# Linear attention and a gated MLP on one core: next chunk's x fetched as soon as it is written, first batch in the steady order, its last normalizers inverted on VectorE

## The chip, the cores and the metric

The kernel runs on one core of a Trainium2 chip. The metric is device time in microseconds (us), as the median of several runs; lower is better. A core has a matrix engine (TensorE, PE in the profile; its weight loads are PEld), VectorE (DVE), ScalarE (ACT), GpSimd (POOL) and SyncE (SP), each with an instruction queue of its own that is executed in order. In this kernel SP issues every DMA; a transfer that has to wait for something holds up SP's queue behind it.

## The reference

Attention with a feature map and without a softmax over the sequence, followed by a gated MLP over all tokens. There are 8 batches, 8 heads, 576 positions, head size 64, 128 features; the MLP has 4608 tokens, width 512 and hidden width 1536.

```python
def phi(x):
    proj = np.einsum('bhsd,df->bhsf', x, w_phi)
    proj = proj - np.max(np.abs(proj), axis=-1, keepdims=True)
    return np.concatenate([np.exp(proj), np.exp(-proj)], axis=-1)
q_p, k_p = (phi(q), phi(k))
kv = np.einsum('bhsf,bhsd->bhfd', k_p, v)
z = np.sum(k_p, axis=2)
num = np.einsum('bhsf,bhfd->bhsd', q_p, kv)
den = np.einsum('bhsf,bhf->bhs', q_p, z)[..., None] + 1e-06
attn = num / den
...
gate = 1.0 / (1.0 + np.exp(-(x @ w_gate)))
val = x @ w_val
out = gate * val @ w_out
```

Here x is attn with the heads of a token side by side (4608 x 512).

## The kernel before

The first part of the program does the attention and a third of the MLP side by side; the second part does the other two thirds of the MLP and is not touched by the change.

**Attention.** Two heads make a pair, so there are 32 pairs, four to a batch. For each pair, `keys` and `rest` project k on PE, `k_exp` takes the maxima and differences on DVE and the exponentials on ACT; `q_half` projects q in two halves, `q_max` finds each position's maximum on DVE (a reduction with a transpose, some small copies and a transpose back) and subtracts it, `q_exp` exponentiates on ACT; `kv` multiplies the keys' features by v and sums them, `turn` transposes the result, and `num` (L569 to L596) computes numerators (`nm`) and denominators (`dp`). `norm` (L598 to L634) then inverts the denominators: a DMA gathers them into a tile of 128 x 9 (`dn`), DVE adds 1e-6 and inverts, a DMA writes them to DRAM (`den`), two DMAs read them back spread over all partitions (`rb`), DVE multiplies (`xp`), and the product goes to DRAM in the layout of x (`xscr`, shown as `xs`). For the first batch `norm` also splits the product into a high and a low part, straight into the x tiles of chunks 0 and 1 in SBUF.

**The MLP's first third.** The tokens are cut into 18 chunks of 256, and the hidden width into 12 blocks, of which this part does four. For each chunk c and block i, `half(c, i, m)` does the 12 matmuls of the gate (m = 0) or of the value (m = 1) into a `gv` bank; each product of two f32 values is made of three matmuls of high and low parts. `gate` makes the hidden tile, and `half_out` multiplies it by the output weights. From chunk 2 on, `load_x` (L202 to L211) reads the chunk's x from `xscr` by one DMA into the low tile, waits three ticks, casts the high part on ACT (L208), waits one, and subtracts on DVE (L210). There are two sets of x tiles.

**Order.** In this part the order of the instructions on every engine is that of the program. Work that needs several steps is a generator in a list, `tasks`; `start` runs its first step and each `tick` runs one more step of every task in the list, so a `yield` puts later steps behind what other tasks issue. `fill` (L664) is called four times a pair. It makes three ticks, and between them runs as many items of MLP work as its budget allows: what is ready, spread over the calls that are left until more is due, at most `RATE` a call. `queue(b)` enters the chunks that batch b completes, right after the numerators of the batch's last pair, and sets their due call: two calls on for the first batch, eight for the others (`LAG`). At that call the chunks' items join the list of ready work; `chunk(c)` and `first` also enter the chunk in the set `cs`. `begin(c)` (L213) starts `load_x(c)` if c is in `cs` and hasn't been started; it is called at the start of `half`, which then ticks until the x tile is complete, and after the second half of every block but the first, for chunk c+1.

**The first batch** has a loop of its own (L709 to L740): for pair i it projects keys and queries of pair i+1, then does `q_exp`, `kv`, `turn` and `num` of pair i one after another. The later pairs run in the loop at L742, where `num(i-1)` stands between `kv(i)` and `turn(i)`.

**Weights** come as 64-bit floats and are taken apart on DVE and ACT, twelve tiles in this part; `grant(n)` lets the task `weigh` go on up to tile n, and `need` makes `half` wait for the tile it reads.

Of the kernel before, what the change touches and what calls it, by code (L numbers as in the profile page):

```python
# [36 lines left out]
EARLY = NP  # L37
RATE = 2.8
LAG = (2, 8)
TICKS = 3  # L40


@with_exitstack
def attention_moe(
# [144 lines left out]
    def start(g):  # L189

        if next(g, tasks) is not tasks:
            tasks.append(g)

    def tick():
        for g in list(tasks):
            if next(g, tasks) is tasks:
                tasks.remove(g)

    def half_units(js, mp, ps_gv, ps_acc, need):
        xs, hs, gvs, cs, parts = {}, {}, {}, set(), collections.Counter()  # L200

        def load_x(c):  # L202
            xh, xl, raw = x_tiles(mp, CH, f"1_{c}")
            xs[c] = xh, xl
            nc.sync.dma_start(raw, xscr[c])
            for _ in range(3):
                yield
            act.copy(xh, raw)  # L208
            yield
            vec.tensor_tensor(xl, raw, xh.bitcast(F32), op=ALU.subtract)  # L210
            parts[c] = NP  # L211

        def begin(c):  # L213
            if c in cs and c not in xs:
                start(load_x(c))

        def gate(c, i, n):
            gv = gvs.pop((c, i))
            u = mp.tile([P, CH], F32, tag="u", name="u" + n)
            t = mp.tile([P, CH], F32, tag="t", name="t" + n)  # L220
            hh = mp.tile([P, CH], F32R, tag="hh", name="hh" + n, bufs=10)
            hl = mp.tile([P, CH], F32R, tag="hl", name="hl" + n, bufs=10)
            hs[c, i] = hh, hl, None
            act.activation(t, gv[:, 0, :], AF.Tanh, scale=0.5)
            act.activation(u, gv[:, 0, :], AF.Exp)
            yield
            tu = t.bitcast(U32)
            vec.tensor_scalar(tu, tu, 0x7FFFFFFF, None, op0=ALU.bitwise_and)
            vec.scalar_tensor_tensor(t, t, 1.0, gv[:, 1, :], op0=ALU.add, op1=ALU.mult)
            vec.scalar_tensor_tensor(u, u, 1.0, t, op0=ALU.min, op1=ALU.mult)  # L230
            yield
            act.copy(hh, u)  # L232
            yield
            vec.tensor_tensor(hl, u, hh.bitcast(F32), op=ALU.subtract)  # L234
            parts["h", c] += 1

        def half(c, i, m):
            begin(c)
            while parts[c] < NP:
                tick()  # L240
            need(js[i], m)
            n = f"1_{c}_{js[i]}"
            if m == 0:
                gvs[c, i] = ps_gv.tile([P, 2, CH], F32, tag="gv", name="gv" + n)
            mm_in(gvs[c, i][:, m, :], xs[c], js[i], m, CH)
            if m == 1:
                start(gate(c, i, n))
                if i >= 1:
                    begin(c + 1)

        def half_out(c, t):
            need(js[-1], 2)
            while parts["h", c] < len(js):
                tick()
            acc = ps_acc.tile([P, DM], F32, tag="acc", name=f"acc1_{c}_{t}")
            for i, j in enumerate(js):
                mm_out(acc, t, hs[c, i], j, i == 0, i == len(js) - 1)
            y = mp.tile([P, DM], F32, tag="y", name=f"y1_{c}_{t}")
            act.activation(y, acc, AF.Copy, scale=0.5)

            def store():
                yield
                nc.sync.dma_start(yscr[c][t], y)

            start(store())

        def unit(c, i):
            return [(1.45, lambda m=m: half(c, i, m)) for m in range(2)]

        def chunk(c):  # L270

            cs.add(c)
            items = []
            for i in range(len(js)):
                items += unit(c, i)
                if i < 2:
                    items += outs(c - 1)[i : i + 1]
            return items

        def first():  # L280

            cs.update((0, 1))
            items = []
            for i in range(len(js)):
                items += unit(0, i) + unit(1, i)
            return items + outs(0)

        def outs(c):
            return [(0.69 * len(js), lambda t=t: half_out(c, t)) for t in range(2)]

        return chunk, first, outs, xs, parts

    def rest_chunks(js, xp, mp, ps_gv, ps_acc, load):
        def load_x(C):
# [57 lines left out]
    with ExitStack() as actx:  # L352
# [9 lines left out]
        def bank(shape, name):  # L362
            return ps_a.tile(shape, F32, tag="a", name=name)
# [202 lines left out]
                yield  # L566
            exps[i] = es

        def num(i):  # L569
            es, w = exps.pop(i), kvs.pop(i)  # L570
            ex = at.tile([P, S], F32, tag="ex", name=f"ex{i}")
            nms = [bank([P, HS], f"nm{i}_{hf}") for hf in range(2)]
            dp = bank([P, HS], f"dp{i}")
            for hf in range(2):
                cs = slice(hf * HS, hf * HS + HS)
                for sg in range(2):
                    for o in range(0, P, Q):
                        nc.tensor.matmul(  # L578
                            nms[hf][o : o + Q, :], w[:, sg, o : o + Q],
                            es[sg][:, o // D, cs],  # L580
                            start=sg == 0, stop=sg == 1, tile_position=(0, o),
                        )
            for sg in range(2):
                for o in range(0, P, Q):
                    hd, hf = divmod(o // Q, 2)
                    z = (2 * hd + sg) * Q
                    nc.tensor.matmul(  # L587
                        dp[o : o + Q, :], w[:, 2, z : z + Q],
                        es[sg][:, hd, hf * HS : hf * HS + HS],
                        start=sg == 0, stop=sg == 1, tile_position=(0, o),  # L590
                    )
            dr = at.tile([P, HS], F32, tag="dr", name=f"dr{i}", bufs=1)
            for hf in range(2):
                act.copy(ex[:, hf * HS : hf * HS + HS], nms[hf])
            act.copy(dr, dp)
            start(norm(i, ex, dr))  # L596

        def norm(i, ex, dr):  # L598
            b, p = steps[i]
            dn = at.tile([P, 9], F32, tag="dn", name=f"dn{i}")  # L600
            rb = at.tile([P, S], F32, tag="rb", name=f"rb{i}", bufs=1)
            yield
# [5 lines left out]
            yield  # L608
            nc.sync.dma_start(dens[i].rearrange("h (r c) -> (h r) c", c=9), dn)
            yield  # L610
            for hd in range(2):
                nc.sync.dma_start(
                    rb[head(hd), :], dens[i][hd].unsqueeze(0).broadcast_to([D, S])
                )
            for _ in range(3):
                yield
            xp = at.tile([P, S], F32, tag="xp", name=f"xp{i}")
            vec.tensor_tensor(xp, ex, rb, op=ALU.mult)
            for c in range(S // CH if b == 0 else 0):
# [8 lines left out]
            while t < S:  # L628
                c, o = divmod(b * S + t, CH)
                w = min(CH - o, S - t)  # L630
                nc.sync.dma_start(
                    xscr[c][:, p * CH + o : p * CH + o + w], xp[:, t : t + w]
                )
                t += w  # L634

        weighed = []
# [4 lines left out]
                grant(3 * j + m + 1)  # L641
                tick()

        chunk, first, outs, xs, parts = half_units(list(range(JA)), moe, ps_gv, ps_acc, need)
        ready, coming = [], []
        cdone = wdone = spot = after = 0
        wq = []
# [16 lines left out]
        def fill(n=TICKS):  # L664
            nonlocal due, spot, after
            spot += 1
            while coming and coming[0][0] <= spot:
                b, cs = coming.pop(0)[1:]
                after = spot + 4 * NP + (0 if b else 6 + LAG[1] - LAG[0])
                if b == 0:  # L670
                    ready.extend(first())
                else:
                    for c in cs:
                        ready.extend(chunk(c))
# [31 lines left out]
            load_v(i)  # L706
        start(weigh())

        keys(0)  # L709
        copies(q_half(0, 0))  # L710
        tick()
        copies(q_half(0, 1))
        rest(0)
        start(q_max(0))
        for _ in range(4):
            tick()
        for i in range(EARLY):
            more = i + 1 < EARLY
            if more:
                keys(i + 1)  # L720
                copies(q_half(i + 1, 0))
            start(q_exp(i))
            tick()
            tick()
            kv(i)
            tick()
            if more:
                copies(q_half(i + 1, 1))
                rest(i + 1)
                start(q_max(i + 1))  # L730
            tick()
            turn(i)
            load(i + 2)
            load_v(i + 2)
            tick()
            tick()
            num(i)
            tick()
            tick()
            grant((0, 1, 2, 6)[i])  # L740
        queue(0)
        for i in range(EARLY - 1, N + 1):  # L742
            if EARLY <= i:
# [108 lines left out]
```

## Time and profile before

| What | us |
|---|---|
| median of 3 runs (1372.89 to 1375.34) | 1373.25 |
| the profiled execution, whole | 1375.71 |
| its span in the profile | 1373.9 |
| TensorE busy | 1240.4 |
| VectorE busy | 793.9 |
| ScalarE busy | 528.5 |

The profile is that of one execution, and its times of instructions belong to that one. A busy line gives an engine's time and its share of the span. Lines of a timeline give the start, the time, the engine, the line of the program, the operation and the tiles written and read, with the number of instructions merged; in square brackets stands how long the engine had been idle before, and what ended that idle time. A line of waits gives an engine and line, the engine and line it waited for, the total, the number of waits and the longest. The granted clock is the share of full speed at which TensorE was let run; 1.00 is full.

### The profile page before, as it was taken

What the parts mean: (1) busy time and instruction counts of PE and PEld (TensorE: products, weight loads), DVE (VectorE), ACT (ScalarE), POOL (GpSimd) and SP (SyncE); (2) the same over time, 40 slices, a digit from 0 to 9 for tenths busy, and PEclk for the clock granted to TensorE, in tenths of its full rate; (3) what the DMA queues carried; (4) which work ended last, traced back from release to release, by engine and by line L of the source; (5) the groups of instructions that cost most, each with busy time, mean ns of one, the idle gap of its engine ahead of it and who ended that gap; (6) DMA issues with size and microseconds to landing.
All of it is one profiled execution on the core that took longest, in us unless ns stands there. A gap on an engine that the chain in (4) does not pass through costs nothing.

```text
span 1373.9 us, 22434 instructions
## 1 busy us (share of the span) xinstructions
PE 1240.4 (90%) x9104; PEld 975.0 (71%) x9104; DVE 793.9 (58%) x1606; ACT 528.5 (38%) x1082; POOL 0.7 (0%) x6
## 2 busy tenths in 40 slices
PE   6656986979979999797987999999999999999998
PEld 4334654757757777575687888888888888888887
DVE  6689774875858777587279495243434343424333
ACT  5435554645535565463444342221212221212211
POOL 0000000000000000000000000000000000000000
PEclk9968898989989999898999999999999999999999
DMA  4566232323323333232276362020202020201010
GB/s 152 170 227 206 93 107 92 116 88 100 117 79 112 113 117 100 76 112 66 67 240 209 129 207 92 0 93 1 92 0 92 0 93 1 92 26 67 1 62 31
DMA packets 81303, 131.84 MB, mean 96 GB/s; under 512 B 18608, under 2 KB 38192, under 8 KB 81200
## 3 DMA queue, kind: packets, MB, share of 16 engines
q1 hardware_dynamic: 81200, 130.41, 29.0%
q8 instruction: 72, 1.18, 0.4%
q14 instruction: 31, 0.25, 0.1%
HBM read 92.33 MB, written 28.46 MB: 88 GB/s over the span
## 4 chain that ended last, share of the span: by engine, by line
PE 70%; DVE 17%; DMA 7%; ACT 3%; issue 2%; SPq 1%; DVEq 0%
PE acc L170 19%; PE g L163 14%; PE v L163 14%; PE gv L163 10%; PE kvz L528 3%; PE nm L578 3%; DMA den<-dn 2%; DMA rb<-den 2%; PE dp L587 2%; DMA wraw<-w_moe 2%; DVE d L518 2%; PE pq L411 1%; DVE pm L500 1%; DVE mb L513 1%; PE pk L421 1%
## 5 line engine op out<-in xcount | busy, mean ns | idle before, releaser
L163 PE MATMUL gv<-xh,wh 128*128 128x256 f32 x576 | 178.3, 310 | 47.0 <-ACT xh L208 24.8
L163 PE MATMUL gv<-xl,wh 128*128 128x256 f32 x576 | 171.7, 298 | 28.1 <-DVE xl L210 28.1
L170 PE MATMUL acc<-wh,hh 128*128 128x512 f32 x432 | 172.8, 400 | 1.7 <-ACT hh L232 1.0
L163 PE MATMUL gv<-xh,wl 128*128 128x256 f32 x576 | 170.9, 297 | 0.0
L170 PE MATMUL acc<-wh,hl 128*128 128x512 f32 x432 | 169.1, 391 | 1.1 <-DVE hl L234 0.9
L170 PE MATMUL acc<-wl,hh 128*128 128x512 f32 x432 | 169.3, 392 | 0.0
L163 PEld LDWEIGHTS gv<-xh,wh 128*128 128x128 f32 x576 | 117.8, 205 | 65.5 <-ACT xh L208 25.8
L163 PEld LDWEIGHTS gv<-xl,wh 128*128 128x128 f32 x576 | 118.0, 205 | 30.3 <-DVE xl L210 29.7
L61 ACT CAST hh<-u 128x512 fp32r<-128x512 f32 x72 | 44.7, 621 | 228.4 <-DVE u L184 228.4
L182 DVE TENSOR_SCALAR t<-t 128x512 uint32<-128x512 uint32 x72 | 30.6, 426 | 166.9 <-ACT t L179 166.9
L163 PEld LDWEIGHTS gv<-xh,wl 128*128 128x128 f32 x576 | 118.2, 205 | 0.0
L163 PE MATMUL g<-xh,wh 128*128 128x512 f32 x288 | 113.0, 392 | 0.0
L163 PE MATMUL v<-xh,wh 128*128 128x512 f32 x288 | 112.6, 391 | 0.0
L163 PE MATMUL g<-xh,wl 128*128 128x512 f32 x288 | 112.5, 391 | 0.0
L163 PE MATMUL g<-xl,wh 128*128 128x512 f32 x288 | 112.5, 391 | 0.0
L163 PE MATMUL v<-xl,wh 128*128 128x512 f32 x288 | 112.3, 390 | 0.0
L163 PE MATMUL v<-xh,wl 128*128 128x512 f32 x288 | 112.1, 389 | 0.0
L179 ACT ACTIVATE t<-g 128x512 f32<-128x512 f32 x72 | 43.0, 597 | 175.5 <-PE g L163 175.2
L183 DVE SCALAR_TENSOR_TENSOR t<-t,v 128x512 f32<-128x512 f32 x72 | 49.4, 686 | 96.5 <-PE v L163 96.5
L170 PEld LDWEIGHTS acc<-wh,hh 128*128 128x128 f32 x432 | 81.4, 188 | 24.3 <-issue 4.8
L170 PEld LDWEIGHTS acc<-wh,hl 128*128 128x128 f32 x432 | 81.3, 188 | 21.0 <-DVE hl L234 2.5
L454 ACT ACTIVATE ek<-dk 128x512 f32<-128x512 f32 (+1 forms) x192 | 87.6, 519 | 19.6 <-DVE dk L445 18.8
(90 smaller groups left out, 2106.0 us busy)
## 6 DMA issues: line engine op xcount, KB each, us to landing
wraw<-w_moe SPq DMA_DIRECT2D x36, 512.0 KB
xl<-xs SPq DMA_DIRECT2D x34, 512.0 KB
k<-k SPq DMA_DIRECT2D x32, 320.0 KB
v<-v SPq DMA_DIRECT2D x32, 320.0 KB
q<-q SPq DMA_DIRECT2D x32, 288.0 KB
rb<-den SPq DMA_DIRECT2D x64, 144.0 KB
wh<-wtop SPq DMA_DIRECT2D x36, 256.0 KB
ys<-y SPq DMA_DIRECT2D x36, 256.0 KB
```

What stands on the lines that cost most here:

```text
L61: a = act.copy(h, x)
L163: nc.tensor.matmul(o, a[:, ws], x[:, cs], start=i == 0, stop=i == 11)
L170: nc.tensor.matmul(acc, a[:, ts], w[:, ws], start=first and i == 0, stop=last and i == 2)
L179: act.activation(t, g, AF.Tanh, scale=0.5)
L182: vec.tensor_scalar(tu, tu, 0x7FFFFFFF, None, op0=ALU.bitwise_and)
L183: vec.scalar_tensor_tensor(t, t, 1.0, vl, op0=ALU.add, op1=ALU.mult)
L411: nc.tensor.matmul(pps[hd], wk[head(hd), :], x[head(hd), cs], start=True, stop=True)
L454: act.activation(e[:, :, sg * F : sg * F + F], dk, AF.Exp, scale=1.0 - 2.0 * sg)
L518: vec.tensor_tensor(d, d, mb, op=ALU.subtract)
L528: nc.tensor.matmul(kvz[o : o + Q, : 2 * F], vx[:, 2 * t + hd, o % D : o % D + Q], (e0, e1)[hd][:, t, :] if t < 4 else e2[:, 0, :], start=t ...
L578: nc.tensor.matmul(nms[hf][o : o + Q, :], w[:, sg, o : o + Q], es[sg][:, o // D, cs], start=sg == 0, stop=sg == 1, tile_position=(0, o),)
L587: nc.tensor.matmul(dp[o : o + Q, :], w[:, 2, z : z + Q], es[sg][:, hd, hf * HS : hf * HS + HS], start=sg == 0, stop=sg == 1, tile_position ...
```

## The change

It has three parts. First, `begin` no longer looks at the set `cs`: it starts a chunk's load as soon as the whole chunk has been written to `xscr` (counted at the stores, in `parts["x", c]`) and chunk c-2, whose x tiles it takes, has had all its matmuls issued (`parts["v", c-2]`). `fill` calls it from three calls ahead of the due call (`AHEAD`), `half` calls it for c+1 after every block, and the loop that ticks until x is complete calls it too. Second, the first batch's loop takes the order of the later pairs: `num(i-1)` between `kv(i)` and `turn(i)`. Third, the last pair of the first batch, `num(3, True)`, makes its denominators for both halves in every row (two banks in place of one), adds 1e-6 and inverts them on DVE over 128 x 576, and goes straight to the product, without the three DMAs. For all other pairs `norm` reads `rb` one tick later and multiplies two ticks later than before, and `ex` has three buffers in place of two.

```diff
+AHEAD = 3
...
         def begin(c):
-            if c in cs and c not in xs:
+            free = c < 2 or parts["v", c - 2] == len(js)
+            if c not in xs and free and parts["x", c] == CH * NP:
                 start(load_x(c))
...
         def half(c, i, m):
-            begin(c)
             while parts[c] < NP:
+                begin(c)
                 tick()
...
             if m == 1:
+                parts["v", c] += 1
                 start(gate(c, i, n))
-                if i >= 1:
-                    begin(c + 1)
+                begin(c + 1)
...
-        def num(i):
+        def num(i, soon=False):
...
-            ex = at.tile([P, S], F32, tag="ex", name=f"ex{i}")
+            ex = at.tile([P, S], F32, tag="ex", name=f"ex{i}", bufs=3)
             nms = [bank([P, HS], f"nm{i}_{hf}") for hf in range(2)]
-            dp = bank([P, HS], f"dp{i}")
+            dps = [bank([P, HS], f"dp{i}_{hf}") for hf in range(1 + soon)]
...
+            for n, dp in enumerate(dps):
+                for sg in range(2):
+                    for o in range(0, P, Q):
+                        hd = o // D
+                        hf = n if soon else o // Q % 2
+                        z = (2 * hd + sg) * Q
+                        nc.tensor.matmul(
+                            dp[o : o + Q, :], w[:, 2, z : z + Q],
+                            es[sg][:, hd, hf * HS : hf * HS + HS],
+                            start=sg == 0, stop=sg == 1, tile_position=(0, o),
+                        )
             for hf in range(2):
                 act.copy(ex[:, hf * HS : hf * HS + HS], nms[hf])
-            act.copy(dr, dp)
+            if soon:
+                rb = at.tile([P, S], F32, tag="mb", name=f"rb{i}", bufs=1)
+                for hf, dp in enumerate(dps):
+                    cs = slice(hf * HS, hf * HS + HS)
+                    vec.tensor_scalar(rb[:, cs], dp, 1e-6, None, op0=ALU.add)
+                    vec.reciprocal(rb[:, cs], rb[:, cs])
+                start(scale(i, ex, rb))
+                return
+            dr = at.tile([P, HS], F32, tag="dr", name=f"dr{i}", bufs=1)
+            act.copy(dr, dps[0])
             start(norm(i, ex, dr))
...
             nc.sync.dma_start(dens[i].rearrange("h (r c) -> (h r) c", c=9), dn)
             yield
+            yield
             for hd in range(2):
...
-            for _ in range(3):
+            for _ in range(4):
                 yield
+            yield from scale(i, ex, rb)
+
+        def scale(i, ex, rb):
+            b, p = steps[i]
             xp = at.tile([P, S], F32, tag="xp", name=f"xp{i}")
             vec.tensor_tensor(xp, ex, rb, op=ALU.mult)
...
+                parts["x", c] += w
                 t += w
...
             spot += 1
+            if coming and coming[0][0] <= spot + AHEAD and coming[0][1]:
+                begin(coming[0][2][0])
...
-        keys(0)
-        copies(q_half(0, 0))
...
-        for i in range(EARLY):
...
+        for i in range(-1, EARLY):
+            load(i + 2 if i >= 0 else N)
+            if i + 1 < EARLY:
                 keys(i + 1)
                 copies(q_half(i + 1, 0))
+                tick()
+                tick()
                 copies(q_half(i + 1, 1))
                 rest(i + 1)
                 start(q_max(i + 1))
+                tick()
+                tick()
+            if i >= 0:
+                kv(i)
+                start(q_exp(i))
+            if i >= 1:
+                num(i - 1)
             tick()
             tick()
-            num(i)
+            if i >= 0:
+                turn(i)
+                load_v(i + 2)
             tick()
             tick()
-            grant((0, 1, 2, 6)[i])
+            grant(i)
+        num(EARLY - 1, True)
+        grant(6)
         queue(0)
```

More of the change, by code (lines that the diff above doesn't have):

```diff
@@ L199, in half_units @@
     def half_units(js, mp, ps_gv, ps_acc, need):
-        xs, hs, gvs, cs, parts = {}, {}, {}, set(), collections.Counter()
+        xs, hs, gvs, parts = {}, {}, {}, collections.Counter()
         def load_x(c):
@@ L270, in chunk @@
         def chunk(c):
-            cs.add(c)
             items = []
@@ L280, in first @@
         def first():
-            cs.update((0, 1))
             items = []
@@ L289, in outs @@
             return [(0.69 * len(js), lambda t=t: half_out(c, t)) for t in range(2)]
-        return chunk, first, outs, xs, parts
+        return chunk, first, outs, begin, xs, parts
     def rest_chunks(js, xp, mp, ps_gv, ps_acc, load):
@@ L582, in num @@
                         )
[L583 to L592, printed above, removed]
+            for n, dp in enumerate(dps):
[9 more added lines that the diff above has]
+                        )
             for hf in range(2):
                 act.copy(ex[:, hf * HS : hf * HS + HS], nms[hf])
-            act.copy(dr, dp)
+            if soon:
[8 more added lines that the diff above has]
+            act.copy(dr, dps[0])
             start(norm(i, ex, dr))
         def norm(i, ex, dr):
-            b, p = steps[i]
             dn = at.tile([P, 9], F32, tag="dn", name=f"dn{i}")
@@ L642, in need @@
                 tick()
-        chunk, first, outs, xs, parts = half_units(list(range(JA)), moe, ps_gv, ps_acc, need)
+        chunk, first, outs, begin, xs, parts = half_units(list(range(JA)), moe, ps_gv, ps_acc, need)
         ready, coming = [], []
@@ L707, in attention_moe @@
         start(weigh())
-        keys(0)
-        copies(q_half(0, 0))
[L711 to L716, printed above, removed]
-        for i in range(EARLY):
-            more = i + 1 < EARLY
-            if more:
+        for i in range(-1, EARLY):
+            load(i + 2 if i >= 0 else N)
+            if i + 1 < EARLY:
                 keys(i + 1)
                 copies(q_half(i + 1, 0))
[L722 to L727, printed above, removed]
+                tick()
+                tick()
                 copies(q_half(i + 1, 1))
@@ L730, in attention_moe @@
                 start(q_max(i + 1))
[L731 to L734, printed above, removed]
+                tick()
[5 more added lines that the diff above has]
+                num(i - 1)
             tick()
             tick()
-            num(i)
+            if i >= 0:
+                turn(i)
+                load_v(i + 2)
             tick()
             tick()
-            grant((0, 1, 2, 6)[i])
+            grant(i)
+        num(EARLY - 1, True)
+        grant(6)
         queue(0)
```

## The prediction

> **What bounds the kernel now.** I read the page first, then busy time by stage, then who waits for whom on TensorE, then the timeline of each engine around the longest waits.
>
> ```profile
> span 1373.9 us, 22434 instructions
> PE 1240.4 (90%) x9104; PEld 975.0 (71%) x9104; DVE 793.9 (58%) x1606; ACT 528.5 (38%) x1082; POOL 0.7 (0%) x6
> ```
> ```profile
> 485.40:549.50 64.10, 64.08 (x664) 49.71 (x664) 49.20 (x111) 37.20 (x85) 0.00 (x0) 1.00 0.36 111
> 777.00:1373.90 596.90, 592.64 (x2593) 486.30 (x2591) 245.54 (x394) 144.34 (x235) 0.00 (x0) 1.00 0.18 60
> ```
>
> Columns of the stage view: stretch, length, busy time of PE, PEld, DVE, ACT, POOL, then granted clock, DMA share, GB/s. After 777 PE is full at clock 1.00; the change doesn't touch that stage. Before it, a stretch without waits (485 to 549) is full too, with DVE at 77%. So in the first 777 us time is lost only where PE stands still, or runs slowly after standing still.
>
> ```profile
> PE gv L163 <- DVE xl L210: 28.1, 6, 5.9
> PE gv L163 <- ACT xh L208: 24.8, 5, 7.5
> PE pq L411 <- ACT d L473: 16.5, 8, 5.5
> PE tp L554 <- ACT kvt L547: 13.0, 5, 4.3
> PE gv L163 <- ACT xh L61: 12.1, 1, 12.1
> ```
>
> Those are PE's waits up to 760: total, times, longest. The first two belong together: the two halves of a loaded x tile. The 12.1 is one wait, for the first batch's last pair.
>
> ```profile
> 295.75 0.58 PE L163 MATMUL gv<-xh,wh 128*128 128x256 f32 x1 [4.35 <-ACT xh L208]
> 302.06 0.58 PE L163 MATMUL gv<-xl,wh 128*128 128x256 f32 x1 [5.74 <-DVE xl L210]
> 485.43 0.39 PE L163 MATMUL gv<-xl,wh 128*128 128x256 f32 x1 [1.08 <-DVE xl L210]
> ```
> ```profile
> 295.70:302.00 6.30, 0.58 (x1) 0.29 (x1) 6.07 (x14) 0.00 (x0) 0.00 (x0) 0.50 0.00 1
> ```
>
> One such event: PE waits 4.35 for the high part, runs one matmul, waits 5.74 for the low part, while DVE is busy 6.07 of 6.30 with the next pair's work, which stands ahead of the subtraction in its order. There are five events (five waits of the second kind), each at the first chunk of batches 1, 2, 3, 5 and 6. At chunk 9 (485.43), whose load the loop over chunk 8 had begun ahead, only 1.08 is left: the kernel's own example of what the prefetch does. Five events cost 28.1 + 24.8 - 1.1 = **51.8 us**.
>
> **The change, part by part.** *Early x.* The old rule begins a load only once its chunk is in the list of work, at its due spot. In the new one fill begins it from three spots ahead if the stores are written and the second buffer is free. Counting the code: a pair's stores now come 12 ticks after its numerators (10 before), a fill makes 3 ticks, so they are out at the end of the fourth fill after queue; the chunk is due at the eighth and the load may begin at the fifth. Chunk c-2's last matmuls lie two or more fills before that in every batch from 1 to 6. So all five loads begin three fills early.
>
> ```profile
> 321.48 6.18 DMA xl<-xs
> ```
> ```profile
> 82.42 1.11 SPq L612 DMA_DIRECT2D rb<-den  x2
> 78.14 0.42 SPq L609 DMA_DIRECT2D den<-dn  x1
> ```
> ```profile
> L208 ACT CAST xh<-xl x16: 1028/1045/1057, 213.8 to 744.4; 128x1024 fp32r<-128x1024 f32 x16
> L210 DVE TENSOR_TENSOR xl<-xl,xh x16: 1174/1218/1226, 218.1 to 746.8; 128x1024 fp32r<-128x1024 f32 x16
> ```
>
> The load must wait until the stores have landed. The nearest row is the other write-then-read through DRAM: den issued at 78.14, its reader at 82.42, 4.3 us. Then 6.18 for the load, 1.05 and 1.22 for the split: 12.7 us. By the planner's arithmetic the full stretch, 64.1 us, runs from chunk 9's first half to chunk 11's, 14 fills with what stands between them: 4.6 us a fill, and fills five to seven give 13.7. The x arrives just in time, and the 51.8 goes. Within a batch the next chunk's load begins one unit sooner, where nothing waits today: no term.
>
> The slow clock behind each wait goes too:
>
> ```profile
> 219.40:224.00 4.60, 4.60 (x39) 3.41 (x43) 0.94 (x2) 0.00 (x0) 0.00 (x0) 0.58 0.00 0
> 302.00:308.00 6.00, 5.94 (x55) 5.20 (x59) 1.98 (x6) 0.66 (x2) 0.00 (x0) 0.73 0.00 0
> 388.30:394.00 5.70, 5.66 (x31) 5.22 (x35) 1.01 (x2) 0.35 (x2) 0.00 (x0) 0.51 0.00 0
> 560.20:566.00 5.80, 5.80 (x43) 5.32 (x47) 1.27 (x3) 0.66 (x2) 0.00 (x0) 0.62 0.01 3
> 643.80:650.00 6.20, 6.20 (x35) 5.52 (x39) 1.31 (x4) 0.66 (x2) 0.00 (x0) 0.51 0.01 3
> ```
>
> Busy time by (1 - clock): 1.9 + 1.6 + 2.8 + 2.2 + 3.0 = **11.5 us**. [...]
>
> *What is late next.* During an event DVE ran ahead; without it DVE and PE go side by side.
>
> ```profile
> 553.90:637.50 83.60, 73.32 (x773) 55.75 (x773) 59.45 (x131) 43.95 (x98) 0.00 (x0) 0.93 0.29 93
> 140.60:214.90 74.30, 60.11 (x655) 40.73 (x654) 56.04 (x127) 41.44 (x91) 0.00 (x0) 0.89 0.37 113
> ```
>
> A batch with an event holds 59.45 of DVE in 83.6; shortened by 10.1 + 2.2 that is 83%, a little above the 77% at which PE lost nothing. Bounds for what PE gives back: 0 (485 to 549), and 6.7 per batch (140.6 to 214.9: 14.2 idle, 7.5 of it x), which is 33 for five. I take 1.4 a batch, **7 us**, near the first row, which is the same stage in the same order.
>
> *First batch in the steady order, last normalizer on DVE.*
>
> ```profile
> 53.12 1.14 PE L587 MATMUL dp<-eq,kv 128*32 128x288 f32 x16
> 66.54 1.14 PE L587 MATMUL dp<-eq,kv 128*32 128x288 f32 x16
> 87.60 0.58 PE L163 MATMUL gv<-xh,wh 128*128 128x256 f32 x1 [12.06 <-ACT xh L61]
> ```
> ```profile
> 6.51 1.29 DVE L432 TENSOR_REDUCE mx<-pk 128x4 f32<-128x512 f32 x2 [5.23 <-PE pk L421]
> 70.40 0.76 DVE L618 TENSOR_TENSOR xp<-ex,rb 128x576 f32<-128x576 f32 x1 [9.00 <-DMA rb<-den]
> 75.97 0.17 DVE L606 TENSOR_SCALAR dn<-dn 128x9 f32<-128x9 f32 x1
> 76.17 0.21 DVE L607 RECIPROCAL dn<-dn 128x9 f32<-128x9 f32 x1
> 87.58 0.76 DVE L62 TENSOR_TENSOR xl<-xp,xh 128x256 fp32r<-128x256 f32 x2 [0.47 <-ACT xh L61]
> ```
> ```profile
> 0.00:67.70 67.70, 46.37 (x630) 27.02 (x630) 42.83 (x95) 35.50 (x74) 0.70 (x6) 0.90 0.48 160
> 67.70:91.30 23.60, 9.03 (x50) 7.44 (x50) 18.24 (x41) 7.76 (x18) 0.00 (x0) 0.61 0.57 189
> 91.30:140.60 49.30, 33.92 (x318) 23.57 (x317) 46.27 (x102) 23.92 (x52) 0.00 (x0) 0.85 0.65 220
> ```
>
> Pair 3's denominators end at 67.7, its x is usable at 87.6: 20 us through three transfers (dn, den, rb). The new form puts both halves' denominators into two PSUM banks (16 matmul records more, 1.1 us on PE; four of five banks, so none is waited for beyond today) and adds on DVE two additions and two reciprocals of 128x288. The addition I price by the 0.38 of one 128x256 pass (two in 0.76), 0.4. The reciprocal of 288 isn't in the trace: 0.45 if 9 elements' excess of 0.04 is a fixed cost, 0.4 + 288 x 0.04 / 9 = 1.7 if it is per element. I take 0.45, since a pass of that width is the nearer row, and keep 2.5 us (two of them) for the range. [...]
>
> With pair 3 short, **pair 2 is late next**: it keeps its three transfers and is now normalized 11 ticks after its numerators, beyond num(3). Today its way from 54.3 to 71.2 takes 17 us. Started some 3 us earlier, since num(i-1) now fills PE's wait between kv and turn, it ends near 68, against 87.6: up to 20 us on PE.
>
> But DVE can't follow that far. From 67.7 to 140.6 it is busy 64.5 of 72.9 with weights, keys and maxima; the 12 us wait on PE was covered work for it. So the stage is worth what DVE idles: 24.9 + 5.4 + 3.0 = 33.3. Of that 6.5 at the start stays; the 9.0 for pair 2's rb I halve; the other 17.8 I halve too (the new order removes PE's waits for kvt, not ACT's copies). Left 19.9, gain 13.4, less 1.3 added work: **12 us**. Bounds: 4 (only part of the 9.0 goes) and 20 (PE's own).
>
> *Small moves.* Two more ticks in norm put rb's load behind one more tick of SP's queue (k and q loads stand there) and the product later: DVE's waits for rb shrink, off PE's path. A third ex buffer covers the longer life. Weights are granted at the same pairs as before, only the third to sixth in two steps about num(3): no term. At the end:
>
> ```profile
> 691.94 1.27 SPq L631 DMA_DIRECT2D xs<-xp  x3
> 693.46 0.32 SPq L205 DMA_DIRECT2D xl<-xs  x1
> ```
>
> Batch 7 never reaches its due spot minus three; chunk 15's load comes with a later half of chunk 14, about one unit, under 3 us; I take **1 us** lost, 0 to 3.
>
> **Sum.** The profiled execution took 1375.7 (span and 1.8 around it): 1375.7 - 51.8 - 11.5 + 7 - 12 + 1 = 1308.4. It stands 2.5 above the median 1373.25, so I forecast **1306**.
>
> **Rivals.** (a) *DVE takes x's place*: 83% busy and in order, it holds PE 6.7 a batch as from 140 to 215, 26 us more: 1332. For it: that row. Against: 485 to 549. 15%. (b) *The first batch gives all that PE could take*, DVE being refilled: 8 more from the start, nothing given back: 1291. 10%. (c) *The prefetch doesn't fire ahead*, because the stores are a tick short of the fifth fill: only the first batch's 12 less 1 remain: 1373.25 - 11 = 1362. The count above has no slack but is exact. 4%. (d) *Slower*: ACT's cast of x stands three ticks behind its load in ACT's in-order queue, SP's load directly behind the store; behind them ACT owes kv copies and gates to PE, SP the next dn and rb. If each of the 16 loads holds PE for its 6.18, that is 99 us against 67 won: 1373 + 32 = 1405. It decides from 67 / 16 = 4.2 us a load. Against it: chunk 9 lost 1.08 with such an early load. [...] 4%.
>
> **Chances.** Forecast 67%, own range 1294 to 1320 (first batch 4 to 20, reciprocals, tail). The range goes to (b) and (a): 1290 to 1334, leaving out (c), (d) and tails. Faster (over 0.2%, about what a measurement of this kernel can tell) 0.95, same 0.01, slower 0.04.
>
> **What would show it.** No PE wait for xh L208 or xl L210 above 2 us, x loads issued some 12 us before their first matmul; clock 1.00 from 220 to 640; the first gv without a 12 us gap, and rb of pair 2 as what it waits for; DVE near full to 125. Wrong would be: new PE waits for d, dk or kvt beyond 7 us in that stage, ACT waiting for x loads, or RECIPROCAL near 2 us.

## The result, and the profile after

The changed kernel takes 1298.51 us (median of 4 runs, 1296.95 to 1299.89) against 1374.30 for the kernel before: a ratio of 0.9449, 95% interval 0.9431 to 0.9466. In a later comparison it was 0.9432 (0.9408 to 0.9456). The forecast was 1306, with a range of 1290 to 1334. The profiled executions stand 78.3 us apart, 1375.71 and 1297.41.

The page of the changed kernel opens so:

```profile
span 1295.6 us, 22470 instructions
PE 1228.6 (95%) x9120; PEld 970.1 (75%) x9120; DVE 797.9 (62%) x1608; ACT 526.8 (41%) x1081; POOL 0.7 (0%) x6
```

To see where the 78.3 lie, I cut both executions at the same three instructions of PE: the second q projection of the twelfth pair (pair 11, counted from 0; the expectations below wrongly call it pair 9), the numerators of the last pair, and the first matmul of the untouched second part. Stage view, first the kernel before, then the changed one; columns as in the prediction (busy time of PE, PEld, DVE, ACT and POOL, then granted clock, DMA share and GB/s):

```profile
0.00:206.09 206.09, 148.22 (x1643) 98.18 (x1643) 157.65 (x348) 104.05 (x226) 0.70 (x6) 0.86 0.48 159
206.09:672.25 466.16, 408.04 (x4270) 310.10 (x4270) 320.06 (x703) 240.66 (x538) 0.00 (x0) 0.93 0.31 98
672.25:776.92 104.67, 91.44 (x601) 80.37 (x602) 70.64 (x162) 39.47 (x85) 0.00 (x0) 0.93 0.50 167
```
```profile
0.00:199.18 199.18, 151.38 (x1658) 103.83 (x1658) 164.06 (x352) 104.68 (x226) 0.70 (x6) 0.85 0.51 166
199.18:596.03 396.85, 394.35 (x4270) 300.65 (x4271) 317.44 (x701) 237.76 (x537) 0.00 (x0) 1.00 0.37 113
596.03:698.58 102.55, 90.18 (x601) 79.21 (x602) 70.76 (x162) 39.88 (x85) 0.00 (x0) 0.93 0.51 173
```

The first stretch became 6.9 us shorter, the second 69.3, the third 2.1. In the second the same 4270 matmul records now take 394 us of 397, at a clock of 1.00: PE's idle time fell from 58.1 to 2.5 (55.6 us), and the rest, 13.7, is matmuls that ran faster. DVE is busy for 80% of it, and still PE stands idle for only 2.5 us.

Who PE waited for in the changed kernel, up to 710 us, five rows of the list (total, times, longest):

```profile
PE pq L411 <- ACT d L473: 17.6, 7, 5.0
PE gv L164 <- ACT xh L62: 11.9, 2, 8.4
PE gv L164 <- ACT xh L209: 2.9, 1, 2.9
PE gv L164 <- DVE xl L211: 2.8, 1, 2.8
PE tp L554 <- ACT kvt L547: 1.8, 2, 1.1
```

L209 and L211 are the two halves of a loaded x (L208 and L210 before). Of 52.9 us 5.7 are left, all of it at chunk 15 near the end. The waits for kvt went too, from 13.0 to 1.8; the list of early x alone still has 11.0 of them and that of the first batch alone 4.0 (both runs follow below), so most of this belongs to the steady order. It isn't all won: waits of `kvz` that the profile puts to no releaser ("issue") are 6.8 in the changed kernel, where the one wait of `kvz` before was 3.1. The first batch's wait for xh is hardly shorter than it was, 11.9 in place of 12.1.

### The profile page after: what moved, and what is told of

Read it like the earlier page. It is cut to its first block, busy times and chain, and to the rows that moved or that the text cites. A ratio compares the mean times of both kernels' runs of the same rounds, so it can differ in the third digit from the quotient of the medians.

```text
span 1295.6 us, 22470 instructions
## 1 busy us (share of the span) xinstructions
PE 1228.6 (95%) x9120; PEld 970.1 (75%) x9120; DVE 797.9 (62%) x1608; ACT 526.8 (41%) x1081; POOL 0.7 (0%) x6
## 4 chain that ended last, share of the span: by engine, by line
PE 81%; DVE 11%; ACT 3%; issue 2%; DMA 2%; SPq 0%; DVEq 0%; ACTq 0%
PE acc L171 21%; PE g L164 15%; PE v L164 15%; PE gv L164 12%; PE kvz L528 5%; PE nm L580 4%; PE pq L411 2%; PE dp L591 2%; PE pk L421 2%; ACT eq L564 1%; PE kvz L542 1%; DMA wraw<-w_moe 1%; PE pk L482 1%; DVE mb L513 1%; PE tp L554 1%
## 5 line engine op out<-in xcount | busy, mean ns | idle before, releaser
L164 PE MATMUL gv<-xh,wh 128*128 128x256 f32 x576 | 174.5, 303 | 17.0 <-ACT xh L62 11.9
L164 PE MATMUL gv<-xl,wh 128*128 128x256 f32 x576 | 167.2, 290 | 2.8 <-DVE xl L211 2.8
L164 PE MATMUL gv<-xh,wl 128*128 128x256 f32 x576 | 166.5, 289 | 0.0
L164 PEld LDWEIGHTS gv<-xh,wh 128*128 128x128 f32 x576 | 114.1, 198 | 34.6 <-issue 14.9
L164 PEld LDWEIGHTS gv<-xl,wh 128*128 128x128 f32 x576 | 114.1, 198 | 3.9 <-DVE xl L211 3.0
L164 PEld LDWEIGHTS gv<-xh,wl 128*128 128x128 f32 x576 | 114.0, 198 | 0.0
L171 PEld LDWEIGHTS acc<-wl,hh 128*128 128x128 f32 x432 | 81.3, 188 | 15.8
```

Of the source, the lines that this page charges most:

```text
L164: nc.tensor.matmul(o, a[:, ws], x[:, cs], start=i == 0, stop=i == 11)
L171: nc.tensor.matmul(acc, a[:, ts], w[:, ws], start=first and i == 0, stop=last and i == 2)
```

## The experiments

All are runs of variants on the chip, each compared with runs of the kernel before on the same chip. Where variants are compared with one another, I use these ratios, since the kernel before read 1374 to 1377 from one comparison to the next. The changed kernel is 0.9449.

**Early x alone.** The kernel before with only this:

```diff
+            free = c < 2 or parts["v", c - 2] == len(js)
-            if c in cs and c not in xs:
+            if c not in xs and free and parts["x", c] == CH * NP:
...
+            if coming and coming[0][0] <= spot + AHEAD and coming[0][1]:
+                begin(coming[0][2][0])
```

> Early x alone on the kernel before: its first batch, its normalizers and its ticks are kept, only the rule of begin and the calls of it are the new ones. Theory: the stretch after the first batch gained 69.3 us (206.1 to 672.3 before, 199.2 to 596.0 after) and all of it is early x, nothing of it the first batch or the ticks, and the end another 2: about 1303 us, PE without x waits from 220 on, the 12 us wait for xh of the first batch still there. Rival: the two more ticks in norm are needed too, because DVE waited 20 us for rb in that stretch and once x is early such a wait reaches PE: 1313 or more, with PE waits for d, dk or kvt in the middle.

Measured: 1303.64 (1300.85 to 1306.94), ratio 0.9477 (0.9448 to 0.9506). Its stage view between about the same two points, and PE's wait of the first batch:

```profile
205.60:603.00 397.40, 393.93 (x4281) 300.25 (x4282) 317.24 (x703) 240.44 (x538) 0.00 (x0) 1.00 0.37 114
```
```profile
PE gv L164 <- ACT xh L62: 11.7, 1, 11.7
```

The middle stretch is as full as in the changed kernel, without the two more ticks and without the new first batch. The theory holds: 0.9477 is some 72 us of the 76, and the middle stretch belongs to early x alone.

**First batch alone.** The kernel before with the steady order, the inversion on DVE and the third ex buffer; `begin` and norm's ticks as before.

> First batch alone on the kernel before: steady order, last normalizers on DVE, third ex buffer; the old rule of begin and the old ticks. Theory: the gain is the 6.9 us that the two traces show up to the second q projection of pair 9: about 1367 us, with the five x waits as before (some 52 us). Rival: the first batch is worth the 12 that were forecast and early x shared the rest: 1362.

Measured: 1369.98 (1368.04 to 1373.37), ratio 0.9960 (0.9946 to 0.9975), so 5.5 us (3.4 to 7.4). PE's waits for x are those of the kernel before:

```profile
PE gv L164 <- DVE xl L211: 28.4, 6, 5.9
PE gv L164 <- ACT xh L209: 24.6, 5, 7.2
```

The first batch is worth 3 to 7 us, not 12. With early x alone (72) it makes up the whole of the change, 76.

**Old ticks.** The changed kernel with norm's yields as before.

```diff
             yield
-            yield
             for hd in range(2):
...
-            for _ in range(4):
+            for _ in range(3):
```

> The changed kernel with norm's old ticks: rb one tick sooner, the product two sooner. Theory: no part of the gain, within 2 us of the changed kernel (1298.5), perhaps 1 to 2 below it because the first batch's pairs 1 and 2 come two ticks sooner in DVE's order. Rival: the later product is what keeps DVE from waiting for rb, and without it 5 us or more return: 1304 and above.

Measured: 1301.71, ratio 0.9459 (0.9438 to 0.9481): not to be told from the changed kernel. No gain from the ticks is shown, and early x alone and the first batch alone, both with the old ticks, leave none to explain.

**Less lead.** `AHEAD = 0` in the changed kernel.

> The changed kernel with AHEAD 0: fill begins a load only at its due call, the calls from half stay. Counting the code, the first chunk of batch 1 is then begun at its due call, that of batches 2, 3, 5 and 6 two calls ahead by a half of the chunk before. Theory: x lies ready long before it is used (after: load of chunk 4 issued at 261.0, both parts ready at 267.2), so two calls are enough and only batch 1's wait comes back, 11.3 and 2 for the slow clock: about 1311. Rival, the prediction's step that x arrives just in time (12.7 us needed, 13.7 given): each of the other four loses one call of 4.6 too: about 1330.

Measured: 1310.07 (1309.00 to 1314.71), ratio 0.9528 (0.9503 to 0.9553). In its timeline of PE only the first chunk of batch 1 waits again:

```profile
207.37 0.58 PE L164 MATMUL gv<-xh,wh 128*128 128x256 f32 x1 [6.83 <-ACT xh L209]
212.61 0.58 PE L164 MATMUL gv<-xl,wh 128*128 128x256 f32 x1 [4.66 <-DVE xl L211]
```

Its profiled span is 13.3 longer than the changed kernel's (1308.9 against 1295.6): 11.5 of wait, and the slow clock behind it (0.56 from 212.6 to 218.6, where a 128x256 matmul takes 0.41 us against 0.28 from 222.4 on; an estimated 2.6 by busy time times 1 - clock). The four batches with two calls of lead lose nothing. Why, the changed kernel's timelines of SP, ACT, DVE and PE around chunk 4 show, in this order:

```profile
259.39 1.28 SPq L647 DMA_DIRECT2D xs<-xp  x3
260.99 0.32 SPq L206 DMA_DIRECT2D xl<-xs  x1
```
```profile
264.78 1.05 ACT L209 CAST xh<-xl 128x1024 fp32r<-128x1024 f32 x1 [1.15 <-DMA xl<-xs]
```
```profile
266.02 1.18 DVE L211 TENSOR_TENSOR xl<-xl,xh 128x1024 fp32r<-128x1024 f32 x1
```
```profile
272.05 0.36 PE L164 MATMUL gv<-xh,wh 128*128 128x256 f32 x1
```

The load is issued 1.6 us after the first store, it lands by 264.8, and both parts are ready at 267.2: 7.8 us from store to use, and PE comes 4.9 later.

**Pair 3 through DRAM.** The changed kernel with `num(EARLY - 1)` for `num(EARLY - 1, True)`; run twice.

> The changed kernel with pair 3 of the first batch normalized through DRAM like the others; the steady order and early x stay. Theory: DVE is the bound of the first 140 us, and the new form costs it 4.7 us (two passes of 0.4 and two reciprocals of 1.95) where the old one costs 0.4; but pair 3's product then stands 11 ticks after its numerators, behind weights and maxima that DVE does first, and PE waits for it: 3 to 8 us slower than the changed kernel, 1302 to 1306. Rival: DVE's saved 4.3 us count more than the place, since pair 2 was late anyway: 1294 to 1297.

> The changed kernel with pair 3 normalized through DRAM, again. Earlier it came out 0.0028 of the time before below the changed kernel, with intervals that touch. Theory now: the inversion on DVE is worth nothing or costs up to 4 us, because the first 140 us are bound by DVE and the transfers cost DVE nothing: 0 to 4 us below the changed kernel. Rival: the earlier result was scatter and the inversion wins the 2 to 8 us that its shorter way promises: above the changed kernel.

> The changed kernel again, beside the next three on one chip: 1298 to 1302, ratio to before 0.943 to 0.947. In this comparison it is what the others are held against, since single executions of one kernel differ by 3 us and more in the first 200 us.

Measured: first 1296.77, ratio 0.9421 (0.9402 to 0.9439); in the second comparison 1296.61 and 0.9421 (0.9399 to 0.9444), beside 1298.39 and 0.9432 (0.9408 to 0.9456) for the changed kernel on the same chip. My first expectation, 3 to 8 us slower, was a miss. Both times the variant came out lower, by 3.9 us (ratios) and 1.8 us (medians), within overlapping intervals: the inversion on VectorE brings nothing that these runs show. Yet PE waits more in it. Its timeline of PE, the three waits for the first batch's pairs 1, 2 and 3:

```profile
69.29 0.58 PE L164 MATMUL gv<-xh,wh 128*128 128x256 f32 x1 [3.64 <-ACT xh L62]
79.03 0.58 PE L164 MATMUL gv<-xh,wh 128*128 128x256 f32 x1 [8.48 <-ACT xh L62]
87.81 0.58 PE L164 MATMUL gv<-xh,wh 128*128 128x256 f32 x1 [7.53 <-ACT xh L62]
```

19.7 us of waiting against 11.9, and no loss: these waits of PE aren't what ends the stage.

**Without the reciprocals.** In the changed kernel each of the two is replaced by one integer pass that approximates the inverse:

```diff
-                    vec.reciprocal(rb[:, cs], rb[:, cs])
+                    bits = rb[:, cs].bitcast(U32)
+                    vec.tensor_scalar(bits, bits, -1.0, 2129859011.0, op0=ALU.mult, op1=ALU.add)
```

> The changed kernel with the two reciprocals of pair 3 replaced by one integer pass each that approximates the inverse (its output differs). Theory: the reciprocals took 1.95 us each in place of the 0.45 of the prediction and stand on DVE's saturated way, so about 3 us come off: the second q projection of pair 9 at 196 in place of 199.2, 1295.5. Rival: DVE isn't the bound, PE waits for pair 2's rb: no change, 1298.5.

Measured: 1294.75 (1291.41 to 1296.93), ratio 0.9408 (0.9389 to 0.9426); by the ratios 5.6 us below the changed kernel's 0.9449, with intervals that lie just apart; against its second reading, 0.9432, it is 3.3 us, and the intervals overlap. The pass and what it replaces, from the timelines of DVE of this variant and of the changed kernel:

```profile
61.17 0.31 DVE L604 TENSOR_SCALAR rb<-rb 128x288 uint32<-128x288 uint32 x1
```
```profile
62.27 0.46 DVE L602 TENSOR_SCALAR rb<-dp 128x288 f32<-128x288 f32 x1 [3.46 <-PE dp L591]
62.77 1.95 DVE L603 RECIPROCAL rb<-rb 128x288 f32<-128x288 f32 x1
65.06 1.95 DVE L603 RECIPROCAL rb<-rb 128x288 f32<-128x288 f32 x1
73.88 0.75 DVE L634 TENSOR_TENSOR xp<-ex,rb 128x576 f32<-128x576 f32 x1
83.54 0.75 DVE L634 TENSOR_TENSOR xp<-ex,rb 128x576 f32<-128x576 f32 x1
```

The second q projection of pair 11 in this variant, then in the changed kernel, from the timelines of PE:

```profile
195.57 1.32 PE L411 MATMUL pq<-q,wk 64*128 64x288 f32 x2 [2.28 <-ACT d L473]
```
```profile
199.18 0.75 PE L411 MATMUL pq<-q,wk 64*128 64x288 f32 x2 [2.28 <-ACT d L473]
```

Two reciprocals are 3.9 us of DVE, the two passes 0.6: 3.3 saved, and that projection comes 3.6 sooner, as expected. PE's waits for xh are no shorter in it (13.0 us, against 11.9). Together with pair 3 through DRAM, this speaks for DVE as what bounds the stage and against the rival. These are single executions, and the two of pair 3 through DRAM differ by 3.1 us at the same point (200.51 and 197.37), so the size isn't settled. In the lines of DVE above, the last two are the products of pairs 1 and 2. There is no idle time in brackets before them: DVE came to them when its order came to them, not when a transfer landed.

**Short ticks for the first batch alone.** The old yields where `i < EARLY`.

> The changed kernel with the old ticks in norm for the first batch alone. Theory: PE's two waits for xh of the first batch (3.5 and 8.4) are for pairs 1 and 2, whose products stand late in DVE's order, not for a transfer (DVE had no idle time before them); two ticks sooner they lose 3 to 5 us of it, but DVE then does that much later what it did first, so the total gains 1 to 3: 1295.5 to 1297.5. Rival: the transfer of rb (issued at 74.7) is what is late; DVE then waits for it and nothing is gained or up to 2 lost.

Measured: 1299.20 (1298.39 to 1300.23), ratio 0.9443 (0.9429 to 0.9457). No change. PE's longest wait there stayed, at 8.5 us; the one of 3.5 went, and still the run gained nothing, which is the rival's time; whether by its reason (the transfer late) this run doesn't show, and in the changed kernel's timeline DVE's order came first.

**Pair 2 on DVE as well.** `num(i - 1, i == EARLY - 1)` in the first batch's loop.

> The changed kernel with pair 2 normalized on DVE as well as pair 3. Theory: PE's wait of 8.4 for pair 2 goes, but DVE does 4.3 us more in the stage that it bounds, part of it in the 3.5 and 2.9 us that it idles between 53 and 62: between 2 us better and 2 us worse, 1296.5 to 1300.5. Rival: PE's wait is what counts, 6 us or more better: 1292 or less.

Measured: 1303.36 (1298.64 to 1306.79), ratio 0.9470 (0.9444 to 0.9496), 3 us above the changed kernel by the ratios, though the intervals overlap. The median lies above the 1296.5 to 1300.5 that I expected, so the expectation missed, on the other side from the rival's 1292. PE's wait for pair 2's xh went (one of 3.5 is left), and another took its place. PE's waits up to 200, and the timeline of ACT:

```profile
PE nm L580 <- ACT kv L556: 9.1, 1, 9.1
```
```profile
61.29 0.71 ACT L62 CAST xh<-xp 128x256 fp32r<-128x256 f32 x2 [6.21 <-DVE xp L634]
63.49 2.21 ACT L564 ACTIVATE eq<-d 128x1152 f32<-128x1152 f32 x2
65.60 0.46 ACT L556 COPY kv<-tp 128x384 f32<-128x384 f32 x1
```

ACT's cast waits 6.2 us for DVE's product, and behind it in ACT's order stand the exponentials and the copy that PE needs for pair 3.

**Weights sooner.** `grant(i + 1)` for `grant(i)` in the first batch, in the changed kernel and with pair 3 through DRAM.

> The changed kernel with every weight tile of the first batch granted one pair sooner. Theory: DVE idles some 21 us in the first 63 and is full afterwards; one weight tile (2.6 us of DVE) moves forward into that idle time: 2 to 3 us below the changed kernel. Rival: the weight work then stands before the keys and maxima of the first batch on DVE and ACT and delays them by as much: same or 2 us above.

> Both: pair 3 through DRAM, weights one pair sooner. Theory: the two add, since both take work from DVE's full stretch (4.3 and 2.6 us): 3 to 6 us below the changed kernel, 1293 to 1296. Rival: with PE's wait for pair 3's transfer now ruling, DVE's relief isn't used: as with the first alone.

Measured: 1298.26, ratio 0.9434 (0.9410 to 0.9458), and 1295.56, ratio 0.9409 (0.9383 to 0.9435), beside the changed kernel's 0.9432 on the same chip. The first gave nothing; the second has the lowest median of the four of that comparison, but its interval overlaps the others'. Moving one weight forward wasn't the free fill of DVE's idle time that I took it for. In the trace of the first, pair 11's second q projection comes at 197.54, 1.6 us sooner than in the changed kernel, but the last pair's numerators are level (595.93 and 596.03): what it won at the start was gone by there. The second has the lowest median of the variants that keep the reciprocals; that it beats the changed kernel isn't shown.

## Why the prediction was right, point by point

**What bounds the kernel: right.** Time was lost where PE stood still, and it came back there. The second part took 597.0 us before and after.

**Early x, the idle time: right.** 51.8 was forecast; the middle stretch's idle time fell by 55.6. Early x alone gives it. The load does fire ahead in all five batches, as the count of ticks said.

**"The x arrives just in time": wrong in size.** I needed 12.7 us: 4.3 from store to load, by the den and rb pair, 6.18 for the load, 2.3 for the split. The chain measured 7.8, and 4.9 were left over. The store was followed after 1.6 us and the load landed in under 4, and two calls of lead are enough. The 4.3 was one of the long ones: in the kernel before, rb follows den by 1.4 to 4.6 us over the 32 pairs, with a median of 1.8. And the lines at 691.94 and 693.46 that the prediction shows for the end are a store and a load of the very kind that it wanted to price, 1.5 us apart. The total didn't suffer, since x was in time either way.

**The slow clock: right, and larger.** 11.5 forecast from the five stretches behind the waits, 13.7 measured as PE's busy time saved on the same 4270 records (408.0 at a clock of 0.93 before, 394.4 at 1.00 changed).

**What PE gives back: the step that failed, on the safe side.** I took 7, from DVE at 83% of a shortened batch. Measured: DVE at 80% of 396.85 us, and PE idle for 2.5 in all. The stretch from 485 to 549 had shown it at 77%; in the row of 140 to 215, which I took as the other bound, DVE is busy for less, 75%, so DVE's share isn't what tells the two apart. That row has 97 matmuls of the MLP's gv in 74.3 us, the other 191 in 64.1, and its waits beyond x are for d (4.3) and dk (2.3). That less MLP work between the steps of attention is the reason fits, but no run tested it. Rival (a) stood on that row.

**The first batch: right in mechanism, too large in size.** Forecast 12, measured 6.9 between the traces and 3 to 7 alone. That DVE, not PE, sets this stage was the right step, as far as the runs go: without the reciprocals it is shorter, with 8 us more of PE waiting it isn't longer. But two of its terms were off. The changed kernel's stage view up to the end of the q projection near which the prediction's rows end (137.4 here; before it ends at 140.2, and the prediction's last row runs on for 0.4):

```profile
0.00:53.30 53.30, 42.42 (x545) 28.55 (x549) 38.86 (x87) 29.72 (x63) 0.70 (x6) 0.90 0.48 167
53.30:62.30 9.00, 5.82 (x95) 2.97 (x91) 2.50 (x8) 5.09 (x9) 0.00 (x0) 1.00 0.66 218
62.30:137.40 75.10, 46.55 (x381) 32.22 (x373) 70.05 (x147) 31.93 (x71) 0.00 (x0) 0.72 0.60 201
```

DVE idles 26.0 of 137.4 here, against 33.3 of 140.2: 7.3 less, where I had 13.4. Its work grew from 107.0 to 111.4, by 4.4, where I had 1.3. The second is the reciprocal: 1.95 us each in place of 0.45. I had to choose whether nine elements' excess of 0.04 over an addition is fixed or per element; the 1.95 of 288 elements lies above even the price per element, and the value kept as the other end, 1.7, was the near one. The first is the halving of the idle time, which was a guess: where the wait of 9.0 for rb stood, the second row has 6.5 of 9.0 us idle again, 3.5 of them a wait for pair 3's denominators. So 2.8 of the 6.9 stand at this point. The other 4.1 came later, between 137 and 199, where I had nothing, and they go with the ticks: from this projection to pair 11's, the nine traces with the first batch's longer ticks take 60.9 to 63.8 us, the five with the old ones 64.1 to 66.7. In the trace of the first batch alone, with the old ticks, pair 11's projection comes at 203.66, only 2.4 sooner than before. Yet the totals of the two runs with the old ticks there are not to be told from the changed kernel's, so what the ticks win in this stretch isn't shown to reach the end.

**"Pair 2 is late next": right, for another reason.** PE did wait for it, 8.4 us, until 84.8 rather than the 68 that I worked out from its transfers. Its product stood behind pair 3's reciprocals, pair 1's product, weights and the next pair's maxima in DVE's order.

**The end: wrong by 3 us.** Forecast 1 lost, measured 2.1 gained. Chunk 15 does wait, 2.9 and 2.8. But PE's waits for the gate's t on DVE fell from 10.1 (2.54, 3.95 and 3.64 in the trace before) to 2.2. The gain belongs to early x: from the last pair's numerators to the second part early x alone takes 102.1 us and the first batch alone 104.3, against 104.7 before and 102.6 changed. Chunk 15's wait belongs to the longer ticks: the lists of the two runs that have early x with the old ones everywhere hold none for a loaded x, and there the end takes 102.1 and 101.4.

**The rivals.** (c) fell by the count and by the trace. (d) fell: ACT waited 9.6 us in all for x loads in five places, and PE waited for that cast at one place, the end. (b), 1291, is as far from 1298.5 as the forecast, and half of it holds: nothing was given back in the middle, but the first batch gave less, not more. The misses had opposite signs: +7.0 from the give-back, +3.8 from idle time beyond the five events, +2.2 from the clock, +3.1 at the end, -5.1 from the first batch. They make the 11.0 us between 1308.4, forecast for the profiled execution, and 1297.4. That the first batch's miss took back a third of the others is luck: had it given its 12, the time would have been about 1293, near the lower end of the range.

**The signs.** Three of the signs that the prediction named came out against it, though the time didn't. RECIPROCAL near 2 us was to be a sign of being wrong, and it took 1.95. ACT waiting for x loads was another, and it did, 9.6 us in all. PE's waits for a loaded x were to stay under 2 us, and the two at chunk 15 are above it. In the middle stretch the others held: no wait for x, the clock at 1.00, no wait of PE for d, dk or kvt near 7 us.

## What to carry to other kernels

Where an engine stands still for a load, look for the one place in the same trace where the load happens to come early: it shows what prefetching gives and what the next engine does with the time, better than a bound from another stage. Before shortening a chain of transfers by arithmetic on an engine, see whether that engine bounds the stage: here the arithmetic took 4 us of VectorE and the way through three transfers 0.4 of it (0.17 and 0.21 for the addition and the inverse of nine elements), and the runs show no gain from replacing them, though the waits on the matrix engine promised one. To price a store and the load behind it, look for that same pair in the trace first: it stood there at 1.5 us, while the row taken from another place had 4.3. An operation that occurs only in a tiny form needs a price per element before it is made wide: here 0.21 us at nine elements and 1.95 at 288.

## What the runs showed of the hardware

RECIPROCAL on VectorE took 1.95 us for 288 f32 elements a partition, both times, where the addition from PSUM of that width took 0.46 and 0.39 and, without the reciprocals, the integer multiply-add 0.31. Against the 0.21 of the nine-element form it is (1.95 - 0.21) / 279 = 6.2 ns an element between the two widths.

A load on SP's queue that stands directly behind the store it reads was issued 1.3 to 3.2 us after the store's issue in the changed kernel (seven such pairs; 1.6 for chunk 4). rb followed den by 1.4 to 4.6 us in the kernel before, where SP waited 53.9 us in all for den to land. Both go through DRAM; what makes the long ones long stays open.
